# First unit's diagonal blocks from whole key products, and most gate columns made beside the mixture

## The chip, the cores and the metric

The kernel runs on one core of one Trainium2 chip. The metric is the device time of one execution in microseconds (us), median over runs. TensorE (PE, with its weight loads PEld), VectorE (DVE), ScalarE (ACT) and GpSimd (POOL) compute; SyncE (SP) issues most DMAs.

## What is computed

A linear attention with a delta rule (4 batches, 8 heads, 768 tokens, 48 wide), then a dense layer with a squared rectifier, then a mixture of experts of which each token takes one or none. Only the first two matter here:

```python
k_n = k / (norm(k) + 1e-6)
for t in range(768):
    y[t] = q[t] @ state
    v_old = k_n[t] @ state
    state = state + b[t] * outer(k_n[t], v[t] - v_old)
h = x @ w_in                      # x: 3072 x 384, d_ff 2048
x = (max(h, 0) ** 2) @ w_out      # next: skip and gate scores of x, experts
```

## The kernel before

**Units and chunks.** The sequence is cut into 12 chunks of 64 tokens, two to a unit, six units. In a unit the 16 pairs of head and batch halves and the two chunks make four jobs, `ci` 0 to 3 (two chunks by two halves of heads). For each chunk the recurrence becomes a triangular system of 64x64 per head; its two diagonal blocks of 32x32 are inverted on VectorE for all heads at once (`sysinv`, 31 steps of two operations, L394 and L395, on a tile that has one block per partition), and the off-diagonal block is joined in by small products (`merge`). `recur` then carries the state through the chunks (KS, R, U, Uc, Y, Yc, DS, DSv). Its output `xf` is moved into place by SP (L600) and split into a high and a low half, `xh` (L811) and `xl` (L814), which feed the dense layer. The text calls that layer the mixture: per unit 16 pieces of 128 columns of `w_in`, each a product `h` (L828), activations, and a product `y` (L858).

**The first unit.** Before anything, key and query tiles are loaded (L274). `diag` makes the diagonal blocks straight in PSUM in the layout that a transpose needs: per job 64 small products of a 32-wide block with 16 columns, scattered at a stride of 32 elements, into two banks that stay open over all four jobs. `turn` transposes each bank on VectorE (L359) into `Asys`. `both` makes the products of keys with keys and with queries, and `copy` brings them to SBUF as `G` and `P` on ScalarE (L309, L310). The norms of the keys come from squares on ScalarE (L506), `n2` and `rest` on VectorE (L510 on, tile `nw`), and a multiply on POOL (L519). POOL also masks `P` (L525).

**The weight pieces.** A piece comes as raw 64-bit data (L664) in a ring of four buffers and is converted: `size` on ScalarE (L672), `tail`, `join`, `sign` on VectorE (L676, L681, L685). Then its gate columns, ten more columns of `w_out` times the gate weights, are made: x1 (three transposes, L691), x1c (copy, L695), x2 (three products, L700), x2c (copy, L703). x1c of a piece waits for x2 of the piece before. The opening has nine such pieces, the other seven come in the first unit's mixture. A piece is then split into a high half (L784) and a low half (L788), gate columns included, ahead of its `h`.

**The order.** A planner in the program (`Order`) writes the order of all engines. A job has an urgency (lower goes first), an engine, a planned duration, and jobs that it waits for; each engine takes, among the jobs that are ready within 0.35 us of the earliest, the most urgent. While TensorE has no job in the opening, it puts in dummy products (L1432). The opening is planned until a list of jobs is done (L1460); then the jobs of the mixture are added and planned. Urgencies of the opening: `diag` -400, squares and norms -360 + ci (K0), inversion -350, `both` -200, recurrence R0 = -30 and up, merges MG = -30 + ci, pieces -25 + 2p and up, gate columns at most -10 and up.

Of the kernel before, what the change touches and what calls it, by code (L numbers as in the profile page):

```python
# [8 lines left out]
F32 = mybir.dt.float32  # L9
# [7 lines left out]
PE, ACT, DVE, POOL, SP = ET.PE, ET.Activation, ET.DVE, ET.Pool, ET.SP  # L17
# [2 lines left out]
NO, NR, NQ, CL = 9, 2, 16, 14.0  # L20
GAP = 1.5
U1, V0, C0, CS, CX = 20.0, 0.0, -25.0, 2.0, -10.0
K0, R0, MG = (-360.0, 1.0), (-30.0, 5.0, 2.0), -30.0
S1 = 100.0, 1.0
DL = 3.0
NWR = 6
# [9 lines left out]
B, H, S, D = 4, 8, 768, 48  # L36
# [162 lines left out]
class Attn:  # L199
# [32 lines left out]
    def init(s, pool):  # L232
        s.q0, s.LT0, s.QP0 = ([pool.tile(sh, F32, name=f"{n}0{i}") for i in range(2)] for n, sh in (("gkq", [128, 8, 128]), ("lt", [128, 2, 8, 64]), ("qp", [128, 2, 8, 64])))
        s.Tn0 = pool.tile([128, 32, 32], F32, name="tn0")
        s.one = pool.tile([1, 1], F32, name="root")
        s.nc.vector.memset(s.one, 1.0)
        s.b0 = pool.tile([128, 32], F32, name="b0")
        s.nc.gpsimd.dma_start(out=s.b0, in_=s.bs[0])
# [18 lines left out]
    def gram(s, i, ci):  # L257
        nc = s.nc
        c, h8 = i * 2 + ci // 2, ci % 2 * 8
        st = {}  # L260

        def load():
            st["q"] = s.gq[ci % 2]
            for a in range(2):
                nc.sync.dma_start(out=st["q"][a * 64:a * 64 + D].rearrange("p a b -> p (a b)"), in_=s.kq[c, a, :, h8 * 128:(h8 + 8) * 128])

        if i == 0:
            t = (s.q0[ci] if ci < 2 else s.gq[ci % 2]).rearrange("p a b -> p (a b)")
            kt, qt = (t[:, x * 512:x * 512 + 512] for x in range(2))
            k3, q3 = (x.rearrange("p (a b) -> p a b", b=64) for x in (kt, qt))  # L270

        def load0(x):
            for a in range(2):
                (nc.sync if x or not a else nc.scalar).dma_start(out=(kt, qt)[x][a * 64:a * 64 + D], in_=(s.kf, s.qf)[x][c, a, :, h8 * 64:(h8 + 8) * 64])  # L274

        def diag():
            if ci == 0:
                s.dg = [s.psum([128, 16, 32]) for u in range(2)]
            for p in range(8):
                for a in range(2):  # L280
                    f = 64 - a * 64
                    for j in range(2):
                        o = a * 64 + j * 32
                        for u in range(2):
                            nc.tensor.matmul(s.dg[u][o:o + 32, :, ci * 8 + p], lhsT=k3[f:f + D, p, j * 32:j * 32 + 32], rhs=k3[f:f + D, p, j * 32 + u * 16:j * 32 + u * 16 + 16], start=True, stop=True, tile_position=(f, o))

        def both():
            s.P[0, ci], s.G[0, ci] = s.pP.tile([128, 8, 64], F32, name="P"), s.pG.tile([128, 8, 64], F32, name="G")
            st[0], st[1] = s.psum([128, 4, 128]), s.psum([128, 4, 128])
            for q in range(4):  # L290
                for b in range(2):
                    for x in (k3, q3):
                        for a in range(2):
                            f, o = 64 - a * 64, (x is q3) * 64
                            nc.tensor.matmul(st[b][a * 64:a * 64 + 64, q, o:o + 64], lhsT=k3[f:f + D, 2 * q + b], rhs=x[f:f + D, 2 * q + b], start=True, stop=True, tile_position=(f, a * 64))

        def mm():
            s.P[i, ci] = s.pP.tile([128, 8, 64], F32, name="P")
            s.G[i, ci] = s.pG.tile([128, 8, 64], F32, name="G")
            st[0], st[1] = s.psum([128, 4, 128]), s.psum([128, 4, 128])  # L300
            for q in range(4):
                for b in range(2):
                    for a in range(2):
                        f = (1 - a ^ b) * 64
                        nc.tensor.matmul(st[b][a * 64:a * 64 + 64, q, :], lhsT=st["q"][f:f + D, 2 * q + b, 0:64], rhs=st["q"][f:f + D, 2 * q + b, :], start=True, stop=True, tile_position=(f, a * 64))

        def copy(b):
            P, G, gp = s.P[i, ci], s.G[i, ci], st[b]
            nc.scalar.copy(out=G[:, b::2], in_=gp[:, :, 0:64])  # L309
            nc.scalar.copy(out=P[:, b::2], in_=gp[:, :, 64:128])  # L310

        def store(js=(0, 1)):
            G = s.G[i, ci]
            if i not in s.A:
                s.A[i] = s.dram.tile([128, 32, 32], F32, name="Ad")
            for j in js:
                for a in range(2):
                    r = ((j * 4 + ci) * 2 + a) * 8
                    g = G[a * 64 + j * 32:a * 64 + j * 32 + 32, :, j * 32:j * 32 + 32]
                    nc.sync.dma_start(out=s.A[i][r:r + 8].rearrange("p s t -> s p t"), in_=g)  # L320

        if i == 0:
            return [(SP, 0.5, lambda: load0(0), 0.8), (PE, 2.4, diag, 4, 0, 2) if ci == 0 else (PE, 2.4, diag), (SP, 1.0, lambda: load0(1), 0.8), (PE, 2.0, both, 1, 2048, 2), (ACT, 0.77, lambda: copy(0)), (ACT, 0.77, lambda: copy(1))]
        w, d = (3.6, 2.9) if i == 1 else (1.9, 0.8)
        return [(SP, 1.0, load, 1.3), (PE, 1.0, mm, 1, 1536, 2), (ACT, 0.77, lambda: copy(0)), (ACT, 0.77, lambda: copy(1)), (SP, w, store, d)]

# [16 lines left out]
    def sysinv(s, i):  # L343
        nc = s.nc
        v = nc.vector
        st = {}

        def prep():
            st["A"] = s.c1.tile([128, 32, 32], F32, name="Asys")
            st["b"] = s.p2.tile([128, 32], F32, name="bsys") if i else s.b0  # L350
            st["w"] = s.p2.tile([128, 4, 32], F32, name="wsys")
            if i:
                nc.sync.dma_start(out=st["b"], in_=s.bs[i])
                nc.sync.dma_start(out=st["A"], in_=s.A.pop(i))

        def turn(u):
            if u == 0:
                prep()
            v.transpose(out=st["A"][:, u * 16:u * 16 + 16], in_=s.dg[u])  # L359

        def turn1():
            v.transpose(out=s.Tn0, in_=st["X"].rearrange("p t s -> p s t"))
# [46 lines left out]
        if i:  # L409
            head = [(SP, 1.0, prep, 1.7)]  # L410
        else:
            head = [(DVE, 0.65, lambda u=u: turn(u)) for u in range(2)]
        head += [(DVE, 0.95, n0), (DVE, 0.2, n1), (ACT, 0.25, lambda: st["root"]()), (DVE, 3.1, n2)]
        steps = [(DVE, (0.45 if i else 0.29) + 2 * (31 - k) * (k + 1) / 960, lambda k=k: step(k)) for k in range(31)]
        return head + steps + ([(SP, 0.5, store2, 0.9), (DVE, 1.95, fin1), (SP, 0.5, store1, 1.7)] if i else [(DVE, 1.6, turn1), (DVE, 1.9, turn2)])
# [911 lines left out]
def schedule(A, open_V, open_M, clear, E, free, ca, tail, ew, manual):  # L1327
    o = Order()
    o.use({"a": 3, "y": 4})
    free[0] = o  # L1330
    gr, si, kv, mg, rc = {}, {}, {}, {}, {}


    def at(d, m, *k):
        x = d.get(m)
        for j in k:
            x = x and x[j]
        return [] if x is None else [x]

    def gram(i, c, ul, u, b=()):  # L1340
        m, l = 4 * i + c, A.gram(i, c)
        old = at(gr, m - 2, 5)
        if i == 0:
            x = [o.add(ul + 10, l[2], [], at(gr, m - 1, 0) + list(b))] * 3
            q = o.add(u, l[3], x[:1], at(gr, m - 1, 5) + sd)
            c0 = o.add(u, l[4], [q])
            gr[m] = x + [q, c0, q, o.add(u, l[5], [q, c0])]
            return
        x = [o.add(ul, l[0], old, at(gr, m - 1, 0) + list(b))]
        x += [x[0]] * 2  # L1350
        q = o.add(u, l[1], x[:1], at(gr, m - 1, 5) + at(mg, m - NG, -4) + at(kv, m - NP, 6))
        c0 = o.add(u, l[2], [q])
        c1 = o.add(u, l[3], [q, c0])
        gr[m] = x + [q, c0, q, c1] + [o.add(u, z, [c1]) for z in l[4:]]

    def sysinv(i, u):
        l, x = A.sysinv(i), []
        n = len(l)
        for k in range(n):
            if i == 0:  # L1360
                w = sd[-1:] + x[-1:] if k < 2 else [] if k == 2 else x[-2:] if k == 3 else x[-1:]
            elif k == n - 2:
                w = x[-2:-1]
            else:
                w = x[-1:] if x else [j for c in range(4) for j in gr[4 * i + c][7:]] + at(si, i - 1, -1)
            x.append(o.add(u(k), l[k], w, at(si, i - 1, -2)))
        si[i] = x
# [40 lines left out]
    made, cc, lo = [], [], {}  # L1408
# [21 lines left out]
    with A.tc.tile_pool(name="st", bufs=1, side="right") as pool:  # L1430
# [3 lines left out]
        sd, l0 = [], [A.gram(0, c) for c in range(4)]  # L1434
        ld = []
        for l in l0:
            ld.append(o.add(-400, l[0], [], ld[-1:]))
        o.add(-398, (ACT, 1.5, A.warm), [], ld[-1:])
        for c in range(4):
            sd.append(o.add(-400, l0[c][1], ld[c:c + 1], sd[-1:]))  # L1440
        sysinv(0, lambda k: -350)
        made += [o.add(-140, l) for l in A.init2()]
        for c in range(4):
# [13 lines left out]
        cl = o.add(200, (SP, 0.5, clear, 0.6), [cc[-1][0]], at=170)  # L1457
        for c in range(2):
            keys(1, c, 100 + c, 110 + c)
        o.run(rc[2][2] + rc[3][2] + rc[2][3] + rc[3][3] + [x[-2] for x in cc] + gr[7])  # L1460

    manual.close()
    M = open_M()
# [9 lines left out]
    a = o.taken["a"]  # L1473
# [101 lines left out]
    ld = {}  # L1575
# [60 lines left out]
```

## Time and profile before

| | us |
|---|---|
| median of 3 runs | 894.8 |
| lowest and highest | 889.54, 895.5 |
| profiled execution | 882.78 |
| its span | 881.0 |
| TensorE busy | 831.3 (94%) |
| VectorE busy | 550.2 (62%) |
| ScalarE busy | 489.4 (56%) |
| POOL busy | 205.2 (23%) |

The rows come from one profiled execution, and times in them count from the start of its span. A row of the timeline gives start, duration, engine, source line, operation, output and input tile, and in brackets how long the engine was idle before and what ended that. Matmuls of 32-bit numbers appear as two records each.

### The profile page before, as it was taken

To read this page: it belongs to the slowest core of one execution; us is meant where nothing else is said; L and a number is where in the kernel's file an instruction comes from. 1 tells how busy PE (TensorE), PEld (TensorE's weight loads), DVE (VectorE), ACT (ScalarE), POOL (GpSimd) and SP (SyncE) were. 2 spreads that over 40 slices of the span, in tenths; PEclk is the share of its full clock that TensorE was granted. 3 is DMA by queue.
4 is the path that set the end of the run, shared out by engine and by line. 5 is a ranking of instruction groups with operands and counts; after the bars stand their busy time and mean duration, and the time that the engine had idled before them with its cause. 6 is when DMAs were issued, how large, how long until landed. Compare 5 with 4: busy or idle time off the path is not lost. (4 is left out here: it accounts for less than half of the span.)

```text
span 881.0 us, 24628 instructions
## 1 busy us (share of the span) xinstructions
PE 831.3 (94%) x9410; PEld 722.3 (82%) x9410; DVE 550.2 (62%) x1267; ACT 489.4 (56%) x997; POOL 205.2 (23%) x325
## 2 busy tenths in 40 slices
PE   5988799999999998999999999999999999999996
PEld 4867677887788887888788888898998789998995
DVE  5998899678767885875688543216425226744763
ACT  2448366767556475556765585546643226643651
POOL 6403501132213324232132412002302401111111
PEclk9987599999999998999999999999999999999999
DMA  7446367846675576347663553227702426535661
GB/s 239 161 109 208 112 193 224 237 124 209 176 191 132 152 212 178 106 130 174 186 160 113 155 142 108 96 78 240 275 0 76 140 95 226 208 109 186 215 218 32
DMA packets 112794, 139.24 MB, mean 158 GB/s; under 512 B 65064, under 2 KB 82969, under 8 KB 112656
## 3 DMA queue, kind: packets, MB, share of 16 engines
q1 hardware_dynamic: 103888, 118.15, 45.0%
q0 software_dynamic: 8192, 18.54, 6.6%
q8 instruction: 78, 1.28, 0.6%
q10 hardware_dynamic: 576, 0.79, 0.3%
q14 instruction: 60, 0.49, 0.2%
HBM read 108.55 MB, written 29.88 MB: 157 GB/s over the span
## 5 line engine op out<-in xcount | busy, mean ns | idle before, releaser
L844 DVE TENSOR_TENSOR gl<-g,gh 128x512 fp32r<-128x512 f32 x96 | 67.8, 707 | 114.6 <-ACT gh L837 114.4
L833 ACT ACTIVATE r<-p_h 128x512 f32<-128x512 f32 x96 | 57.3, 597 | 144.1 <-PE p_h L828 144.0
L519 POOL TENSOR_TENSOR x<-x,nw 64x384 f32<-64x384 f32 x48 | 44.5, 926 | 139.8 <-DVE nw L338 131.3
L395 DVE TENSOR_TENSOR Xsys<-Xsys,Osys 128x31 f32<-128x31 f32 (+15 forms) x186 | 69.7, 375 | 6.2
L394 DVE TENSOR_TENSOR Osys<-Asys,Xsys 128x31 f32<-128x31 f32 (+15 forms) x186 | 70.5, 379 | 4.1
L525 POOL TENSOR_SCALAR_AFFINE_SELECT qp<-P 64x512 f32<-64x512 f32 x48 | 37.2, 775 | 133.6 <-PE p_a L592 123.2
L931 POOL DMA_INDIRECT xs<-x2s,di x24 | 25.1, 1046 | 171.6 <-DVE emx L966 65.8
L841 ACT ACTIVATE g<-r 128x512 f32<-128x512 f32 x96 | 60.6, 632 | 6.5 <-DVE gl L844 3.9
L858 PE MATMUL p_y<-wk,gh 128*128 128x394 f32 x288 | 64.2, 345 | 0.0
L828 PE MATMUL p_h<-xh,wk 128*128 128x512 f32 x216 | 63.0, 401 | 0.7 <-DVE wk L788 0.7
L1200 POOL DMA_INDIRECT out<-eo,ex x21 | 23.6, 1123 | 162.8 <-DVEq L1098 94.3
L837 ACT CAST gh<-g 128x512 fp32r<-128x512 f32 x96 | 59.6, 621 | 2.9
L1194 PE MATMUL ey<-w2h,egh 128*128 128x384 f32 x168 | 58.3, 347 | 1.5 <-ACTq L1098 1.3
L1194 PE MATMUL ey<-w2l,egh 128*128 128x384 f32 x168 | 56.6, 337 | 1.5 <-issue 1.5
L858 PE MATMUL p_y<-wraw,gh 128*128 128x394 f32 x240 | 57.6, 362 | 0.0
L828 PE MATMUL p_h<-xh,wraw 128*128 128x512 f32 x180 | 54.6, 411 | 2.7 <-ACT r L833 2.7
L1194 PE MATMUL ey<-w2h,egl 128*128 128x384 f32 x168 | 56.7, 338 | 0.2
L1172 ACT ACTIVATE eg<-eh 128x512 f32<-128x512 f32 x42 | 23.0, 597 | 59.7 <-PE eh L1170 59.3
L858 PE MATMUL p_y<-wraw,gl 128*128 128x394 f32 x240 | 53.6, 346 | 0.0
L858 PEld LDWEIGHTS p_y<-wk,gh 128*128 128x128 f32 x288 | 53.1, 191 | 0.0
L828 PE MATMUL p_h<-xl,wraw 128*128 128x512 f32 x180 | 52.3, 398 | 0.1
L828 PEld LDWEIGHTS p_h<-xh,wk 128*128 128x128 f32 x216 | 41.4, 192 | 10.6 <-DVE wk L788 1.1
(267 smaller groups left out, 1958.0 us busy)
## 6 DMA issues: line engine op xcount, KB each, us to landing
wraw<-wh SPq DMA_DIRECT2D x60, 389.0 KB, 3.7
raw<-in_w SPq DMA_DIRECT2D x16, 768.0 KB, 4.8
r<-in_w SPq DMA_DIRECT2D x24, 512.0 KB, 4.8
r<-in_w SPq DMA_DIRECT2D x32, 384.0 KB, 5.3
wraw<-wc SPq DMA_DIRECT2D x20, 389.0 KB, 3.6
gkq<-in_kq SPq DMA_DIRECT2D x40, 192.0 KB, 3.6
wh<-whi SPq DMA_DIRECT2D x12, 389.0 KB, 3.6
ex<-xs SPq DMA_DIRECT2D x24, 193.0 KB, 2.5
```

Of the source, the lines that this page charges most:

```text
L394: v.tensor_tensor(out=tmp, in0=A[:, k, k + 1:32].unsqueeze(2).to_broadcast(sh), in1=X[:, k, None, 0:k + 1].to_broadcast(sh), op=ALU.mult)
L395: v.tensor_tensor(out=X[:, k + 1:32, 0:k + 1], in0=X[:, k + 1:32, 0:k + 1], in1=tmp, op=ALU.subtract)
L519: nc.gpsimd.tensor_tensor(out=x, in0=x, in1=st["n"][r].unsqueeze(2).to_broadcast([64, 8, D]), op=ALU.mult)
L525: nc.gpsimd.affine_select(out=QP[r, 1 - t], in_=P[r], pattern=[[0, 8], [1, 64]], compare_op=ALU.is_gt, fill=0.0, base=0, channel_multiplie ...
L828: nc.tensor.matmul(ps, lhsT=w[:, k * 128:k * 128 + 128], rhs=x[k], start=(n == 0), stop=(n == 8))
L833: nc.scalar.activation(out=r, in_=st["p"], func=AF.Relu)
L837: nc.scalar.copy(out=s.g[f][0], in_=st["g"])
L841: nc.scalar.activation(out=g, in_=st["r"], func=AF.Square)
L844: nc.vector.tensor_tensor(out=s.g[f][1], in0=st["g"], in1=s.g[f][0].bitcast(F32), op=ALU.subtract)
L858: nc.tensor.matmul(s.ys[t], lhsT=g[:, t * 128:t * 128 + 128], rhs=w[:, DM:], start=first, stop=last)
L931: return s.nc.gpsimd.indirect_dma_start(out=s.xs, out_offset=bass.IndirectOffsetOnAxis(ap=idx, axis=0), in_=src, in_offset=None, bounds_ch ...
L1194: nc.tensor.matmul(y, lhsT=g[:, f, :], rhs=w[:, f, :], start=(i == 0), stop=(i == 23))
```

## The change

The products of the diagonal blocks are gone. `keys` makes the whole 64x64 products of keys with keys of a job; `part(0)` on ScalarE and `part(1)` on VectorE copy the two diagonal blocks of it into an SBUF tile `Gd`, `off` copies the off-diagonal block to `G`; `scores` makes the products with the queries and `copy0` copies them to `P`. `turn` transposes all of `Gd` at once. `keys` and the two parts have urgency -400 + c, `off` -390 + c, `scores` -200 + c. R0 goes from -30 to -40. The opening's list of jobs asks for the sign of all nine pieces and for the gate columns of the first four, where it asked for the gate columns of all nine.

```diff
-K0, R0, MG = (-360.0, 1.0), (-30.0, 5.0, 2.0), -30.0
+K0, R0, MG = (-360.0, 1.0), (-40.0, 5.0, 2.0), -30.0
...
+        s.Gd = pool.tile([128, 32, 32], F32, name="gd")
...
-        def diag():
...
-                        for u in range(2):
-                            nc.tensor.matmul(s.dg[u][o:o + 32, :, ci * 8 + p], lhsT=k3[f:f + D, p, j * 32:j * 32 + 32], rhs=k3[f:f + D, p, j * 32 + u * 16:j * 32 + u * 16 + 16], start=True, stop=True, tile_position=(f, o))
...
+        def keys():
+            st["k"] = s.psum([128, 8, 64])
             for p in range(8):
                 for a in range(2):
                     f = 64 - a * 64
...
+                    nc.tensor.matmul(st["k"][a * 64:a * 64 + 64, p], lhsT=k3[f:f + D, p], rhs=k3[f:f + D, p], start=True, stop=True, tile_position=(f, a * 64))
+
+        def part(j):
+            for a in range(2):
+                o = a * 64 + j * 32
+                (nc.vector.tensor_copy if j else nc.scalar.copy)(out=s.Gd[o:o + 32, ci * 8:ci * 8 + 8], in_=st["k"][o:o + 32, :, j * 32:j * 32 + 32])
+
+        def off():
+            s.G[0, ci] = s.pG.tile([128, 8, 64], F32, name="G")
+            for r in (0, 64):
+                nc.scalar.copy(out=s.G[0, ci][r:r + 32, :, 32:64], in_=st["k"][r:r + 32, :, 32:64])
+
+        def scores():
+            st["s"] = s.psum([128, 8, 64])
...
+        def copy0():
+            s.P[0, ci] = s.pP.tile([128, 8, 64], F32, name="P")
+            nc.scalar.copy(out=s.P[0, ci], in_=st["s"])
...
-            return [(SP, 0.5, lambda: load0(0), 0.8), (PE, 2.4, diag, 4, 0, 2) if ci == 0 else (PE, 2.4, diag), (SP, 1.0, lambda: load0(1), 0.8), (PE, 2.0, both, 1, 2048, 2), (ACT, 0.77, lambda: copy(0)), (ACT, 0.77, lambda: copy(1))]
+            return [(SP, 0.5, lambda: load0(0), 0.8), (SP, 1.0, lambda: load0(1), 0.8), (PE, 1.1, keys, 3, 1024), (ACT, 0.7, lambda: part(0)), (DVE, 0.7, lambda: part(1)), (ACT, 0.7, off), (PE, 1.1, scores, 1, 1024), (ACT, 0.6, copy0)]
...
-        def turn(u):
-            if u == 0:
-                prep()
-            v.transpose(out=st["A"][:, u * 16:u * 16 + 16], in_=s.dg[u])
+        def turn():
+            prep()
+            v.transpose(out=st["A"], in_=s.Gd.rearrange("p s t -> p t s"))
...
-            head = [(DVE, 0.65, lambda u=u: turn(u)) for u in range(2)]
+            head = [(DVE, 1.95, turn)]
...
+        dg = []
         for c in range(4):
-            sd.append(o.add(-400, l0[c][1], ld[c:c + 1], sd[-1:]))
+            l = l0[c]
+            sd.append(o.add(-400 + c, l[2], ld[c:c + 1], sd[-1:]))
+            dg += [o.add(-400 + c, z, sd[-1:]) for z in l[3:5]]
+            of = o.add(-390 + c, l[5], sd[-1:])
...
-        o.run(rc[2][2] + rc[3][2] + rc[2][3] + rc[3][3] + [x[-2] for x in cc] + gr[7])
+        o.run(rc[2][2] + rc[3][2] + rc[2][3] + rc[3][3] + [x[4] for x in cc] + [x[-2] for x in cc[:4]] + gr[7])
```

## Rows read from the trace of the kernel before

**Rows 1.** The page's slices of the span, 40 equal ones, tenths.

```profile
PE   5988799999999998999999999999999999999996
```

**Rows 2.** Windows: stretch, length, busy of PE, PEld, DVE, ACT, POOL, clock, DMA, GB/s.

```profile
22.84:59.06 36.22, 31.16 (x503) 27.52 (x501) 33.78 (x79) 14.09 (x41) 10.11 (x15) 0.96 0.48 128
59.06:91.10 32.04, 27.47 (x716) 23.11 (x714) 27.85 (x49) 24.09 (x59) 11.55 (x19) 0.77 0.56 184
91.10:106.47 15.37, 12.96 (x84) 11.14 (x84) 11.96 (x28) 8.58 (x24) 8.17 (x62) 0.50 0.36 108
106.47:160.00 53.53, 49.45 (x406) 41.52 (x403) 49.79 (x113) 33.48 (x65) 4.62 (x4) 0.96 0.70 202
```

**Rows 3.** TensorE's timeline from 4.5, instruction packets 7.93 to 19.5, window of L295.

```profile
4.58 3.36 PE L285 MATMUL p_a<-gkq 48*32 48x16 f32 x216
10.82 1.95 PE L285 MATMUL p_a<-gkq 48*32 48x16 f32 x128 [2.89 <-issue]
...
q8 instruction: 3, 0.05, 2.0%
...
19.57:24.55 4.98, 4.96 (x88) 4.87 (x89) 1.00 1.02 356
```

**Rows 4.** ScalarE's timeline at 7.8; groups by line (busy us, mean ns), 59 to 91.

```profile
7.78 0.20 ACT L241 ACTIVATE root<-root 1x1 f32<-1x1 f32 x1
...
L595 ACT COPY xf<-p_y 128x512 f32<-128x512 f32 x3 | 1.8, 587 | 0.2
L454 ACT COPY Z<-p_y 32x256 f32<-32x256 f32 x5 | 1.8, 365 | 0.1
```

**Rows 5.** VectorE: norms (window, tile nw), a transpose by line, two in the timeline.

```profile
8.00:23.00 15.00, 6.67 (x24) 1.00 0.85 266
...
L362 DVE STREAM_TRANSPOSE tn<-Xsys 128x1024 f32<-128x1024 f32 x1 | 1.9, 1900 | 0.0
...
22.84 1.31 DVE L359 STREAM_TRANSPOSE Asys<-p_a 128x512 f32<-128x512 f32 x2
```

**Rows 6.** The steps: window of tile Osys, two steps, POOL in the timeline and by line.

```profile
28.64:55.33 26.69, 24.57 (x62) 1.00 0.49 115
...
28.65 0.68 DVE L394 TENSOR_TENSOR Osys<-Asys,Xsys 128x31 f32<-128x31 f32 x1
...
107.03 0.19 DVE L394 TENSOR_TENSOR Osys<-Asys,Xsys 128x31 f32<-128x31 f32 x1
...
23.46 2.47 POOL L519 TENSOR_TENSOR x<-x,nw 64x384 f32<-64x384 f32 x2 [3.16 <-DMA x<-in_kv]
...
28.64 2.78 POOL L525 TENSOR_SCALAR_AFFINE_SELECT qp<-P 64x512 f32<-64x512 f32 x4
...
L519 POOL TENSOR_TENSOR x<-x,nw 64x384 f32<-64x384 f32 x8 | 7.3, 910 | 7.7 <-DVE nw L338 4.2 <-DMA x<-in_kv 3.2
```

**Rows 7.** Window of tile raw on VectorE.

```profile
59.06:91.10 32.04, 19.73 (x24) 0.77 0.56 184
```

**Rows 8.** Timeline of the mixture's start, several engines.

```profile
90.14 0.96 DVE L685 SCALAR_TENSOR_TENSOR wk<-raw,wk 128x768 uint32<-128x768 uint32 x1
...
94.03 0.62 ACT L811 CAST xh<-xf 128x512 fp32r<-128x512 f32 x1 [0.57 <-DMA xf<-xf]
...
99.88 0.96 DVE L788 TENSOR_TENSOR wk<-wk,whi 128x778 fp32r<-128x778 f32 x1
...
106.47 1.65 PE L828 MATMUL p_h<-xh,whi 128*128 128x512 f32 x3
106.65 0.36 DVE L572 TENSOR_TENSOR x<-x,p_a 64x192 f32<-64x192 f32 x1 [3.05 <-PE p_a L565]
...
111.43 0.36 DVE L572 TENSOR_TENSOR x<-x,p_a 64x192 f32<-64x192 f32 x1 [1.33 <-PE p_a L565]
```

**Rows 9.** A later piece's gate columns beside the mixture, TensorE's timeline.

```profile
118.07 0.52 PE L691 MATMUL p_a<-idn,cvo 128*128 128x128 f32 x3 [0.98 <-PE p_y L858]
...
120.49 0.73 PE L700 MATMUL p_a<-sg,cvt 128*128 128x10 f32 x6
```

More of the change, by code (lines that the diff above doesn't have):

```diff
@@ L274, in load0 @@
                 (nc.sync if x or not a else nc.scalar).dma_start(out=(kt, qt)[x][a * 64:a * 64 + D], in_=(s.kf, s.qf)[x][c, a, :, h8 * 64:(h8 + 8) * 64])
-        def diag():
-            if ci == 0:
-                s.dg = [s.psum([128, 16, 32]) for u in range(2)]
+        def keys():
+            st["k"] = s.psum([128, 8, 64])
             for p in range(8):
@@ L281, in diag @@
                     f = 64 - a * 64
-                    for j in range(2):
-                        o = a * 64 + j * 32
-                        for u in range(2):
-                            nc.tensor.matmul(s.dg[u][o:o + 32, :, ci * 8 + p], lhsT=k3[f:f + D, p, j * 32:j * 32 + 32], rhs=k3[f:f + D, p, j * 32 + u * 16:j * 32 + u * 16 + 16], start=True, stop=True, tile_position=(f, o))
[L287 to L295, printed above, removed]
+                    nc.tensor.matmul(st["k"][a * 64:a * 64 + 64, p], lhsT=k3[f:f + D, p], rhs=k3[f:f + D, p], start=True, stop=True, tile_position=(f, a * 64))
[9 more added lines that the diff above has]
+            st["s"] = s.psum([128, 8, 64])
+            for p in range(8):
+                for a in range(2):
+                    f = 64 - a * 64
+                    nc.tensor.matmul(st["s"][a * 64:a * 64 + 64, p], lhsT=k3[f:f + D, p], rhs=q3[f:f + D, p], start=True, stop=True, tile_position=(f, a * 64))
+        def copy0():
+            s.P[0, ci] = s.pP.tile([128, 8, 64], F32, name="P")
+            nc.scalar.copy(out=s.P[0, ci], in_=st["s"])
         def mm():
@@ L1340, in gram @@
     def gram(i, c, ul, u, b=()):
-        m, l = 4 * i + c, A.gram(i, c)
+        m, l = 4 * i + c, A.gram(i, c) if i else [l0[c][1]] + l0[c][6:]
         old = at(gr, m - 2, 5)
         if i == 0:
[L1344 to L1347, printed above, removed]
+            x = [o.add(ul + 10, l[0], [], at(gr, m - 1, 0) + list(b))] * 3
+            q = o.add(u, l[1], x[:1], at(gr, m - 1, 5) + sd)
+            gr[m] = x + [q, q, q, o.add(u, l[2], [q])]
             return
@@ L1360, in sysinv @@
             if i == 0:
-                w = sd[-1:] + x[-1:] if k < 2 else [] if k == 2 else x[-2:] if k == 3 else x[-1:]
+                w = dg if k == 0 else [] if k == 1 else x[-2:] if k == 2 else x[-1:]
             elif k == n - 2:
```

## The prediction

> **What bounds the kernel now.** I read the slices of the span first. TensorE is 90% busy or more nearly everywhere but at the left edge [rows 1]. So what the first 107 us save can reach the end, and work that is moved from there into the rest costs its TensorE time. Then I cut the left edge into stretches by the stage that runs in them [rows 2]. From 22.84 to 59.06 VectorE inverts the first unit's systems (33.78 of 36.22 us busy). From 59.06 to 91.10 the recurrence and the weight pieces run, VectorE 27.85 of 32.04, ScalarE 24.09. From 91.10 to 106.47 nothing is full and the clock is 0.50: the gate columns are made one after another. From 106.47 to 160 the mixture runs with TensorE and VectorE both at 93%. What sets the start of the mixture is VectorE's row of work up to 91.10, and behind it TensorE's row of gate columns.
>
> Third, the diagonal blocks. The 512 small records of L285 are 8.1 us of work, but take from 4.58 to 19.66, because TensorE stops three times, waiting for nothing that the profile names: first after 216 records, in the middle of a job of 128, then after every 128, and the instruction queue brings three packets in that time [rows 3]. So it is out of instructions, not of keys. The transposes begin on VectorE at 22.84 [rows 5].
>
> **The change, part by part.** *The blocks on TensorE.* `diag` goes (512 records), `both` (256) is split into `keys` and `scores`, 128 each. Whole products of this kind took 4.96 us for 88 records [rows 3], 0.056 each, so `keys` is 1.8 us a chunk and four are done by 4.58 + 7.2 = 11.8 at the latest. 216 records ran before the first stop, and `keys` needs 128, so no stop lies on this path. Removed: 19.66 - 11.8 = 7.9 us of TensorE, which is not yet a gain, since others become late.
>
> *The copies.* New on ScalarE per chunk: `part(0)` two copies and `off` two, 32x256 out of PSUM, nearest row 0.37 us, and one 128x512, nearest row 0.59 [rows 4]; on VectorE two of 32x256 from PSUM, which the trace doesn't show; between 0.19 (its 128x31 step) and 0.69 (its transpose of 128x512 out of PSUM, 1.31 for two) [rows 5, 6]; I take 0.37, ScalarE's row of the same shape. By the urgencies in the code ScalarE serves part (-400 + c) and off (-390 + c) before the squares of the key norms (-360 + c), and in the order that readiness gives, twelve copies come before the last `part(0)` ends: 12 x 0.37 = 4.4 us behind the table load and its square root, which end at 7.98 [rows 4]. The turn can start at 12.4, not at 11.8. VectorE's own eight copies (3.0 us, 5.5 at the upper bound) lie in that wait, where it has little else: nothing on the path; without that cover they would cost their 3.0.
>
> *What is now late.* Before, the norms of the keys (`n2`, `rest`) were done while VectorE waited for the blocks: 6.67 us of its work between 8 and 23 [rows 5]. Now the squares stand behind twelve to sixteen copies on ScalarE, so `n2` of chunk 0 can't run before the turn, and being more urgent than the inversion (-360 against -350) the four norms go in between the turn and the early steps. Behind them on VectorE wait the steps, and POOL's multiplies L519 wait for each norm. So they come onto the path in full.
>
> *The turn.* One transpose of 128x1024 instead of two of 128x512: 1.90 by the row of the same size, against 1.3 [rows 5].
>
> *The sum to the end of the inversion.* 12.4 + 1.9 turn + 6.7 norms + 4.5 from turn to first step (from the end of the transposes, 22.84 + 1.31, to 28.65) [rows 5, 6] + 26.7 steps + 3.8 two transposes [rows 5, 6] = 56.0. To this a term for POOL: the step on 128x31 takes 0.68 with POOL's selects beside it and 0.19 without [rows 6]; two of POOL's eight multiplies (0.91 each) came after the turn, at 23.46; the six others now fall into the chain too. Bounds: 0, if they meet operations that they don't delay, and 6 x 0.91 = 5.5, if each is waited for in full; a select cost about 0.5 when it met a step, so half of that would be 3; but some of them meet the other norms, and the 6.67 were measured with multiplies beside them. I take 1.0. End: 57.0 against 59.06, 2 us earlier.
>
> *The recurrence and the pieces.* Before, one of the nine pieces was done ahead of 59.06, eight after it [rows 7]. Now all nine come behind the inversion: eight pieces took 19.73 of VectorE between 59.06 and 91.10 [rows 7], so a ninth is 2.5. The last sign ends at 57.0 + 32.0 + 2.5 = 91.5 against 91.10. R0 from -30 to -40 lets the recurrence's operations go before merges and pieces; it changes who waits, not VectorE's sum. I take it as nothing, since the split of xf (xh) came behind the last sign anyway [rows 8]; if ScalarE starves the pieces' `size` it costs up to the 4.2 us that VectorE idled there.
>
> *The gate columns.* Each is a transpose (0.52), a copy, a product (0.73) and a copy [rows 9], with one buffer between them, so they run one behind the other; at the clock of 0.50 [rows 2] I put a piece at twice 0.52 + 0.73, 2.5 us. No DMA hangs on those of the opening, since their store is empty. The first mixture product waited for them: its inputs were ready when the low half of the first weight was, at 99.88 + 0.96 = 100.84, and it began at 106.47 [rows 8]. With five of nine pieces no longer demanded before it, it can begin 91.5 + 9.74 = 101.2: 5.3 us earlier. Work given back: at that pace 5.3 / 2.5, two pieces, are left by then, 2 x 1.25 = 2.5 us beside the mixture. TensorE gains 2.8. VectorE's waits of 3.05 and 1.33 us for TensorE in that stretch [rows 8] go too: 4.4, less 0.4 for the later sign, 4.0. Both engines are at 93% behind it, so I take the middle: 3.4 us.
>
> The profiled execution took 882.78 us, of which 881.0 span; it would become 879.4. Three executions had a median of 894.8, 12 us above the profiled one, so there the same gain gives 891.4.
>
> **A rule weighed.** VectorE's 128x31 product took 0.68 us beside POOL's select and 0.19 alone [rows 6]. The Trainium skill ("SBUF — State Buffer", section "Who interferes with whom") says that a VectorE instruction with two SBUF inputs and a GpSimd instruction that reads SBUF exclude each other, the loser blocked for the whole instruction, and that one that only writes doesn't count. The rows agree: 0.68 is about the length of one select, 2.78 for four. By the rule each multiply is waited for in full, and the sum would have 5.5 in place of 1.0.
>
> **Rivals.** *B, a gain three times as large.* The norms run before the turn after all, or in waits of the chain (ScalarE faster, or the squares let in). For it: ScalarE is free from 7.98 on [rows 4], and before the change all four norms were done by 23 in the waits of others [rows 5]. Against it: twelve copies of more urgent jobs. Then 6.7 us leave the chain: the inversion ends at 50.3, the last sign at 84.8, the first product at 94.5, 12.0 earlier; less 2.5 on TensorE is 9.5, on VectorE 6.3 + 4.4 = 10.7: 10 us, 884.8. Chance 0.22.
>
> *C, POOL eats it.* All six multiplies are waited for in full: the inversion ends 4.5 later than I say, the sign at 96.0, the first product at 105.7. TensorE gains 0.8 with no piece left, VectorE loses 0.5: 0.2 us, 894.6. For it: 24.57 us of steps in 26.69 [rows 6], some at three times their clean length. Against it: POOL waits for a DMA before its last multiplies. Chance 0.20.
>
> *D, slower: the mixture waits for its weights.* The five late pieces need x1, x1c, x2, x2c, high and low half before their product; these stand in ScalarE's queue among the mixture's own activations. If a piece isn't ready when its turn comes, TensorE stops for a pace of 2.5 us and works 1.25: five pieces are 18.8 us, less the 5.3 gained is 13.5 late, 908.3. It decides from two stopped pieces on (7.5 > 5.3). For it: a later piece's transpose did stop TensorE by 0.98 [rows 9]. Against it: only the fifth piece onward is late, and the products of four pieces stand before it on TensorE. Chance 0.10.
>
> The rest, 0.05, is the planner: the order of all later work is laid out anew from other start times, by some us of either sign.
>
> **The numbers.** My forecast, 891.4, has 0.43, with its own range from 887 to 897 (POOL's term from 0 to 3, the pieces given back from none to five, ScalarE's share). 8 in 10 asks for C whole and most of B: 882 to 899; D and the lower tail of B stay out. About 1% (8.9 us) is what a measurement of this kernel can tell from no change: faster means under 885.9, slower over 903.7. Faster: half of B and more, 0.15, and 0.06 from the forecast and the planner: 0.21. Slower: D, 0.08, and the planner: 0.10. Same: 0.69.
>
> **What would show it.** In the new profile: `keys` without a stop, done by 12; the transpose of 128x1024 at 12 to 13; the four norms behind it and not ahead; first step near 25, not 19; last transpose ending at 55 to 59; last sign at 90 to 93; first mixture product near 101 with two or three transposes of pieces behind it. Wrong at the norms if the first step comes before 21; wrong at POOL's term if steps above 0.6 us number more than twenty; wrong at the gate columns if the first product still waits for them, or if TensorE shows waits of a us and more for the halves of the fifth to ninth weight.

## The result and the profile after

| | before | after |
|---|---|---|
| median of 20 runs each, one chip, us | 889.52 | 896.95 |
| lowest and highest, us | 881.98, 897.19 | 892.75, 901.52 |
| profiled execution, us | 882.78 | 899.56 |
| its span, us | 881.0 | 897.8 |

The changed kernel takes 1.0078 of the time before, 95% interval 1.0055 to 1.0101. In a later run, where before has a median of 899.8, the ratio was 1.0034 [1.0005, 1.0062]. So it is 2 to 7 us slower where the prediction said 3.4 us faster. The move is under 1%, but the sign was wrong. That 896.95 lies in the predicted range of 882 to 899 says little: the prediction started from 894.8, a median of three runs of before, whose median is 889.52 here and 897.8 to 899.8 on the chips of the later runs.

The first part went as predicted. This is the timeline of after, several engines (start, duration, engine, line, operation, tiles, count, idle before with its releaser):

```profile
4.57 3.89 PE L282 MATMUL p_a<-gkq 48*64 48x64 f32 x96
8.29 1.10 PE L282 MATMUL p_y<-gkq 48*64 48x64 f32 x32
...
13.51 1.93 DVE L366 STREAM_TRANSPOSE Asys<-gd 128x1024 f32<-128x1024 f32 x1 [0.86 <-ACT gd L287]
15.58 0.55 DVE L517 TENSOR_REDUCE nw<-sq 128x8 f32<-128x384 f32 x1
...
23.55 0.18 DVE L401 TENSOR_TENSOR Osys<-Asys,Xsys 128x31 f32<-128x31 f32 x1
...
29.57 0.89 DVE L401 TENSOR_TENSOR Osys<-Asys,Xsys 128x135 f32<-128x135 f32 x1
...
55.99 1.91 DVE L373 STREAM_TRANSPOSE Asys<-Xsys 128x1024 f32<-128x1024 f32 x1
```

The 128 whole products run to 9.39 without the stops of [rows 3]. The turn is at 13.51, the norms stand behind it, the first step comes at 23.55, and the last transpose ends at 57.90, 1.2 us earlier than the 59.06 of before [rows 2].

Then the windows (stretch, length, busy of PE, PEld, DVE, ACT, POOL, clock, DMA share, GB/s) show a hole that before doesn't have [rows 2]:

```profile
57.90:70.43 12.53, 11.47 (x296) 9.09 (x298) 10.96 (x16) 11.44 (x32) 0.56 (x1) 0.77 0.04 12
70.43:80.45 10.02, 2.46 (x92) 2.13 (x84) 0.00 (x0) 1.69 (x4) 3.65 (x7) 0.67 0.83 250
80.45:102.53 22.08, 15.18 (x342) 13.39 (x342) 19.39 (x36) 11.86 (x25) 5.61 (x7) 0.59 0.63 202
102.53:113.79 11.26, 8.52 (x42) 7.88 (x43) 9.43 (x28) 6.55 (x19) 10.50 (x65) 0.63 0.33 107
```

From 70.43 to 80.45 VectorE does nothing at all, and the DMA engines, idle in the 12 us before (share 0.04), are 83% busy. The timeline says what it waits for, and what stands behind the waiting instruction:

```profile
70.86 0.81 ACT L447 COPY lt<-Asys 32x256 f32<-32x256 f32 x2
80.51 0.94 ACT L679 ACTIVATE raw<-raw 128x768 f32<-128x768 f32 x1 [8.33 <-DMA raw<-in_w]
...
80.45 0.56 DVE L683 TENSOR_SCALAR raw<-raw 128x768 uint32<-128x768 uint32 x1 [10.03 <-DMA raw<-in_w]
80.93 1.50 DVE L624 TENSOR_TENSOR x<-x,p_a 48x192 f32<-48x192 f32 x4
...
101.25 1.28 DVE L692 SCALAR_TENSOR_TENSOR wk<-raw,wk 128x768 uint32<-128x768 uint32 x1
...
107.77 1.15 ACT L818 CAST xh<-xf 128x512 fp32r<-128x512 f32 x2
...
113.79 1.63 PE L835 MATMUL p_h<-xh,whi 128*128 128x512 f32 x3
```

Four of nine pieces are converted by 70.43, as many as the ring holds. The fifth hasn't been loaded, and the recurrence's own operation (DSv, L624) stands behind the piece's in VectorE's order. Last sign at 102.53 (before 91.10), first mixture product at 113.79 (before 106.47) [rows 8]. Why the loads were late, SP's timeline of after shows:

```profile
48.39 0.45 SPq L361 DMA_DIRECT2D bsys<-in_bs  x1
48.94 1.30 SPq L266 DMA_DIRECT2D gkq<-in_kq  x3
71.70 0.35 SPq L362 DMA_DIRECT2D Asys<-Ad  x1
72.10 12.71 SPq L671 DMA_DIRECT2D raw<-in_w  x5
```

SP stands from 50.2 to 71.70 before the load of the second unit's systems, `Asys`. That load overwrites the tile from which the last `place` copies the first unit's inverses (L447, ending at 71.67 above). SP's waits say so too (who waited for whom: us in total, times, longest):

```profile
SPq L362 <- ACT lt L447: 13.8, 1, 13.8
```

The 7.5 us ahead of that went to the last transpose of the inversion (L373). Five raw loads stand behind the load of Asys and are then issued in one bunch. While VectorE stands, the recurrence's next product on TensorE (KS) waits for the DSv that is queued behind the piece:

```profile
81.33 2.24 PE L572 MATMUL p_y<-x,lt 48*64 48x48 f32 x32 [8.41 <-DVE x L624]
```

SP's row of before:

```profile
61.46 5.38 SPq L664 DMA_DIRECT2D raw<-in_w  x3
66.89 0.44 SPq L353 DMA_DIRECT2D bsys<-in_bs  x1
72.79 0.33 SPq L354 DMA_DIRECT2D Asys<-Ad  x1
73.18 0.41 SPq L664 DMA_DIRECT2D raw<-in_w  x1
```

There SP issued three of the five from 61.46, ahead of bsys and Asys, and one behind; the first had come at 25. In the DMA issues of the stretch (count, KB each, median us from issue to landing), after first, before second:

```profile
raw<-in_w SPq DMA_DIRECT2D x6, 768.0 KB, 12.1
```

```profile
raw<-in_w SPq DMA_DIRECT2D x4, 768.0 KB, 4.3
```

The order was turned by the planner. In the planner's own reckoning (planned times, not those of a trace), before, the stores of the second unit's blocks kept SP busy to 56.5; then the raw loads, far more urgent, were ready first. After, the stores are out by 46.1 and landed at 51.0, which makes `prep` ready, the job with both loads. The first ring buffer is free only at 53.05, so `prep` is taken, though less urgent. The planner knows the stores that Asys needs, but not that its tile is still being read.

### The profile page after: what moved, and what is told of

The parts are those of the page before. It is cut to its first block, busy times and chain, and to the rows that moved or that the text cites. A ratio compares the mean times of both kernels' runs of the same rounds, so it can differ in the third digit from the quotient of the medians.

```text
span 897.8 us, 23901 instructions
## 1 busy us (share of the span) xinstructions
PE 838.9 (93%) x9035; PEld 728.9 (81%) x9035; DVE 556.9 (62%) x1274; ACT 490.5 (55%) x1001; POOL 205.4 (23%) x325
## 3 DMA queue, kind: packets, MB, share of 16 engines
q1 hardware_dynamic: 103888, 118.15, 44.6%
## 5 line engine op out<-in xcount | busy, mean ns | idle before, releaser
L402 DVE TENSOR_TENSOR Xsys<-Xsys,Osys 128x31 f32<-128x31 f32 (+15 forms) x186 | 72.3, 389 | 6.4
L1201 PE MATMUL ey<-w2l,egh 128*128 128x384 f32 x168 | 56.5, 336 | 0.0
```

The source lines that it names most:

```text
L402: v.tensor_tensor(out=X[:, k + 1:32, 0:k + 1], in0=X[:, k + 1:32, 0:k + 1], in1=tmp, op=ALU.subtract)
L1201: nc.tensor.matmul(y, lhsT=g[:, f, :], rhs=w[:, f, :], start=(i == 0), stop=(i == 23))
```

## The experiments

All ratios are against the kernel before on the same chip, with 95% intervals. The runs used three chips: one for e1 to e4, one for e5, e6 and the changed kernel once more, one for e7 to e10. Two kernels on different chips are compared through their ratios; the ratio of one kernel differed between chips by 0.3% (e1 and e10) and 0.4% (the changed kernel). The theory (Q in the quoted texts): SP's order costs the time. The rivals: the gate columns beside the mixture (D), POOL and the norms (C), R0.

**One load later (e1).** The changed kernel; only `prep` moves, behind the raw loads.

```diff
+        for x in cc[4:8]:
+            o.link(si[1][0], x[0])
         cl = o.add(200, (SP, 0.5, clear, 0.6), [cc[-1][0]], at=170)
```

> The changed kernel, with one order more: the load of the second unit's systems (bsys, Asys) is issued only behind the raw loads of the fifth to eighth weight piece. Nothing else moves in the planned order of any engine. Theory Q (SP's queue): the 10.03 us in which VectorE stood before the fifth piece's tail go, the raw loads land 4 to 5 us after their issue again instead of 12, the last sign comes at 92 to 93 instead of 102.5, the first mixture product at 102 to 105 instead of 113.8, and the time falls by 7 to 11 us against the changed kernel: 886 to 890 where before measures 889.5, a ratio of 0.996 to 1.000. Rival D (the gate columns beside the mixture cost the time): the stop goes and the sign comes earlier, but the mixture stands still for its weights, and the ratio stays over 1.004. Rival C (norms and POOL): the sign comes earlier by less than 5 us.

0.9904 [0.9868, 0.9940], median 892.8. Run once more on another chip (e10), 0.9931 [0.9904, 0.9957]. The 10 us stop is gone; SP, VectorE, ScalarE and TensorE in the timeline:

```profile
60.29 5.25 SPq L671 DMA_DIRECT2D raw<-in_w  x3
72.00 9.46 SPq L671 DMA_DIRECT2D raw<-in_w  x3
81.98 0.47 SPq L362 DMA_DIRECT2D Asys<-Ad  x1
...
89.28 0.90 ACT L679 ACTIVATE raw<-raw 128x768 f32<-128x768 f32 x1 [5.96 <-DMA raw<-in_w]
90.20 1.33 ACT L593 COPY x<-p_a 64x192 f32<-64x192 f32 x4
...
95.53 1.29 DVE L692 SCALAR_TENSOR_TENSOR wk<-raw,wk 128x768 uint32<-128x768 uint32 x1
...
109.18 1.63 PE L835 MATMUL p_h<-xh,whi 128*128 128x512 f32 x3
```

The gain is larger than expected (0.996 to 1.000), the stage came later: last sign at 96.82 (93.62 in the second run), not 92 to 93, and first product at 109.18 (105.05), not 102 to 105. So this kernel is 6 to 9 us faster than before although its first product comes near that of before (106.47 and 106.84), once later and once earlier. The loss went with the load's place; by which path the gain over before reaches the end, no run shows. A smaller stop of the same kind is left: ScalarE stands 5.96 us for the ninth raw load, and the recurrence's last copies (L593) stand behind it.

**The second half alone (e2).** Before, with R0 at -40 and the new list.

```diff
-        o.run(... + [x[-2] for x in cc] + gr[7])
+        o.run(... + [x[4] for x in cc] + [x[-2] for x in cc[:4]] + gr[7])
```

> The kernel before with the change's second half alone: the opening ends with the signs of all nine pieces and the gate columns of the first four, and R0 is -40. The diagonal blocks are as before. Theory Q: the raw loads stay ahead of the second unit's load, except for the last piece, so no stop of VectorE; inversion ends at 59, last sign at 90 to 92, first mixture product at 100 to 103 instead of 106.5; TensorE has 2 to 5 pieces' gate columns (1.25 us each) beside the mixture; 2 to 4 us faster than before, ratio 0.995 to 0.998. Rival D: products wait for later weights' halves, stops over 1 us on TensorE between 103 and 130, and the ratio is 1.004 or more. Rival R0 (the reordered recurrence starves the pieces): the last sign is later than 93.

0.9962 [0.9935, 0.9990]. Last sign 91.00, first product 103.47. No stop of TensorE for a weight was over 1.4 us. Rival D is out for this half; R0, which moved with it, is taken alone below.

**The first half alone (e3).** After, with the old list and R0 at -30.

> The changed kernel with the change's second half taken back: all nine pieces' gate columns are demanded before the mixture, R0 is -30; the whole products, copies and the one transpose stay. Theory Q: inversion ends at 57.9 as in the changed kernel, the second unit's load still stands ahead of five raw loads, VectorE stops 8 to 11 us before the fifth piece, last sign at 101 to 103, and the first mixture product, 15 us behind the sign as before, at 114 to 118: ratio 1.008 to 1.014, that is no better than the changed kernel. Rival D: without the late gate columns the loss is gone, ratio 1.000 or less. Rival R0: with -30 the stop before the fifth piece is under 4 us.

1.0114 [1.0081, 1.0148]. Last sign 103.62, first product 120.57, and SP as in after:

```profile
73.03 0.35 SPq L362 DMA_DIRECT2D Asys<-Ad  x1
73.42 11.97 SPq L671 DMA_DIRECT2D raw<-in_w  x5
```

The loss is in this half, though its own inversion ends earlier than before's.

**The first half with one load later (e8).** e3's kernel and e1's two lines.

> The changed kernel's first half alone (whole products, copies, one transpose) with the raw loads first; all nine pieces' gate columns are demanded before the mixture and R0 is -30, as in before. It differs from e3_blocks_only by the order of one load alone, and from e7_r30 by the demanded gate columns alone. Theory Q: e3's ratio of 1.011 falls by the stop of about 10 us, to 0.998 to 1.002, with the inversion at 57.9 and the first product at 104 to 109; the gate columns are then worth the difference to e7_r30, 3 to 7 us. If the stop is not what e3 lost, the ratio stays over 1.006.

0.9988 [0.9961, 1.0015]. The raw loads go first again:

```profile
70.68 6.00 SPq L671 DMA_DIRECT2D raw<-in_w  x2
77.77 0.43 SPq L362 DMA_DIRECT2D Asys<-Ad  x1
```

Against 1.0114 that is 1.26%, 11 us, for the place of one job in SP's order, more than the intervals and the 0.4% between chips. In the orders that the planner writes for e3 and e8, all jobs of all engines stand in the same place over the whole program but this one job on SP; the same holds for the changed kernel and e1. So the cause of the loss is shown by two pairs, and the gate columns are no part of it. By itself the first half, with the loads in time, is worth 1 us, which can't be told from nothing.

**The loads late in the kernel before (e4).** Before, with the raw loads from the fifth piece on behind the second unit's load.

```diff
-        b = [g0]
+        b = [g0] + (si[1][:1] if 4 <= p < NO else [])
```

> The kernel before with one order more: the raw loads of the fifth to ninth piece are issued only behind the load of the second unit's systems, as the changed kernel has it; nothing else of the change. Theory Q: the load of Asys waits on SP for the last copy of the first unit's inverses (72 to 73), five raw loads come bunched behind it and land 8 to 12 us after their issue; VectorE stands 6 to 10 us before the fifth piece; last sign at 97 to 101 instead of 91.1; 5 to 9 us slower than before, ratio 1.006 to 1.010. If SP's queue is not the cause: ratio within 0.997 to 1.003.

0.9966 [0.9932, 1.0000]: a miss. The loads were late as in after (Asys at 73.13, four raw loads in a bunch), and the engines waited for them:

```profile
ACT raw L672 <- DMA raw<-in_w: 5.8, 5, 4.4
DVE raw L676 <- DMA raw<-in_w: 0.3, 1, 0.3
```

Last sign 96.86, first product 110.14, 3.3 us later than in the second trace of before (106.84, on another chip). Yet the time didn't rise. What differs from after: VectorE waited 0.3 us for a raw load and not 10, and its last DSv ended at 90.77 (before 90.48, after 99.56). The edit moved more than SP's row. Here the planner reckons with the late loads and lays out the other engines anew: on VectorE a DSv of the recurrence (L617) now stands ahead of the fifth piece's first step, where in after it stands behind (80.93 above):

```profile
72.03 1.47 DVE L617 TENSOR_TENSOR x<-x,p_y 48x192 f32<-48x192 f32 x4 [2.28 <-PE p_y L609]
79.20 0.56 DVE L676 TENSOR_SCALAR raw<-raw 128x768 uint32<-128x768 uint32 x1 [0.28 <-DMA raw<-in_w]
```

So late loads needn't cost time: here they cost nothing that the runs can tell, in the changed kernel 11 us, with the recurrence queued behind them. That it is the recurrence's delay, rather than the pieces', that reaches the end is argued from this comparison, not shown: no run moved the DSv alone.

**R0 (e7).** e1's kernel with R0 at -30.

> The changed kernel with the raw loads first, and R0 back at -30: the recurrence's operations no longer go before the merges' placing copies. Only R0 differs from e1_loads_first. Theory Q says R0 is no part of the loss: ratio 0.987 to 0.994, last sign within 4 us of 96.8. Rival R0 (the new order of recurrence and merges on ScalarE and TensorE matters by itself): the first mixture product moves by over 4 us from 109.2 and the ratio leaves 0.985 to 0.996.

0.9911 [0.9880, 0.9942], like e1. R0 is no part of the loss. Against e8 it differs by the list alone: 0.9911 to 0.9988, so the gate columns beside the mixture are worth some 7 us here, more than the 3.4 of e2. Why more is open.

**The norms ahead of the turn (e5, e9).** e1's kernel with

```diff
-K0 = (-360.0, 1.0)
+K0 = (-410.0, 1.0)
...
-            of = o.add(-390 + c, l[5], sd[-1:])
+            of = o.add(-340 + c, l[5], sd[-1:])
```

> The changed kernel with the raw loads first (as in e1_loads_first), and the key norms of the first unit put ahead of the later diagonal copies: their urgency from -360 to -410, that of the copies into G from -390 to -340. So ScalarE makes the squares between the copies, and three of the four norms are planned ahead of the turn. Theory N (the norms were 6.7 us of the chain behind the turn, as the prediction says): the turn comes 1 to 2 us later, the first step at 19 to 22, the steps run without norms among them and the last transpose ends at 52 to 55 instead of 57.9; last sign and first product 3 to 5 us earlier than in e1_loads_first; time 2 to 5 us below it, ratio 0.984 to 0.988. Theory P (POOL: its multiplies fall on the steps whatever the order, each waited for): the last transpose ends at 56.5 to 58, and the ratio is that of e1_loads_first, 0.990.

0.9895 [0.9856, 0.9935]. The turn moved to 16.49, the first step to 25.73, the steps ran without norms among them, and the last transpose ended at 55.57 instead of 57.88. Moving the norms there was worth 2.3 us, not 6.7: the steps took 26.1 us from first to last instead of 30.6, but the turn came 3.0 us later, with two of the norms and part of the third ahead of it. The first product came at 100.22, 9 us earlier than in e1, but the time hardly fell, so both were run again on one chip.

> e5_norms_first once more, beside e1_loads_first on one chip. In its trace the first unit's scores are copied at 214.5 against 223.4 in e1_loads_first, 8.9 us earlier, yet the whole span was only 3.5 us shorter, and the ratios were 0.9895 and 0.9904. If the 5.4 us between were lost to chance in the last stage (the experts took 220.8 us behind the last unit there, 214 to 219 elsewhere), this run is 4 to 9 us faster than e10_loads_again, ratio 0.980 to 0.987. If a start that is earlier by 9 us is given back further on whatever the run (a later wait sets the end), it is within 3 us of e10_loads_again again, and its last stage is over 219 us again.

> e1_loads_first once more, as the partner of e9_norms_again on the same chip. Theory Q expects 0.987 to 0.994 again, and the first unit's scores at 222 to 225.

0.9940 [0.9913, 0.9966] and 0.9931 [0.9904, 0.9957]: no difference again. In both profiled executions the norms-first kernel reaches the end of the sixth unit 3 to 8 us ahead and then loses 5 us in the experts (220.8 and 220.5 us to the end, against 215.9 and 215.5). Most of it is lost at one place in both. TensorE at its last expert, norms first (e5, e9), then loads first (e10):

```profile
877.80 0.69 PE L1201 MATMUL ey<-w2h,egh 128*128 128x384 f32 x1 [3.77 <-issue]
```

```profile
879.38 0.47 PE L1201 MATMUL ey<-w2h,egh 128*128 128x384 f32 x1 [4.44 <-ACTq L1268]
```

```profile
878.69 0.41 PE L1201 MATMUL ey<-w2h,egh 128*128 128x384 f32 x1 [0.80 <-ACTq L1105]
```

This is where the program leaves the chain of `If`s. The stop is 0.75 to 1.38 us in the other traces (before, e2 and e4 have another of 1.5 to 1.8 behind it). The last products behind it are slower too, 5.60 us for 23 records at a clock of 0.70 (e9), against 4.31 for 24 at 1.00 (e10; windows, columns as above):

```profile
879.40:885.00 5.60, 5.60 (x23) 5.60 (x24) 0.00 (x0) 0.00 (x0) 0.00 (x0) 0.70 0.02 6
```

```profile
877.90:883.00 5.10, 4.31 (x24) 4.11 (x24) 1.29 (x2) 0.71 (x2) 0.97 (x1) 1.00 0.19 55
```

**The remaining stop of e1 (e6).** e1's kernel with the raw load planned at 4.0 us.

```diff
-        return [(SP, 0.5, load, 2.5)] + wide + ...
+        return [(SP, 0.5, load, 4.0)] + wide + ...
```

> The changed kernel with the raw loads first, and with each raw load given 4.0 us instead of 2.5 in the order's plan. What it changes: ScalarE's first step of the last two pieces (size) is put behind the recurrence's copies, and VectorE's work on them with it. In e1_loads_first ScalarE stood 5.96 us before the ninth piece's size, for its load, with the last copies of the recurrence queued behind it, TensorE stood 4.32 and the last Yc came at 91.6 to 95.0. Theory Q (an in-order queue that stands before a load holds up the recurrence): that wait moves behind the recurrence, the last Yc comes at 88 to 91, xh 3 to 6 us earlier than 103.2, the first product at 104 to 107 and the time is 2 to 5 us below e1_loads_first, ratio 0.984 to 0.989. Rival: the pieces themselves set the first product, not the recurrence: first product at 108 to 110 and a ratio of 0.989 to 0.993.

1.0022 [0.9993, 1.0052], no faster than the changed kernel on the same chip (1.0034): a miss, though the stage did what the theory said. The last Yc came at 89.0 instead of 94.4, the first product at 105.31 instead of 109.18. The gain went at the second unit's start, where the mixture's first product came at 236.84 and in e1 at 229.80, with a wait of its own (SP, then TensorE):

```profile
217.43 7.78 SPq L607 DMA_DIRECT2D xf<-xf  x6
226.40 4.11 SPq L328 DMA_DIRECT2D Ad<-G  x8
233.61 4.08 SPq L266 DMA_DIRECT2D gkq<-in_kq  x4
...
234.82 2.10 PE L313 MATMUL p_a<-gkq 48*64 48x128 f32 x32 [10.36 <-DMA gkq<-in_kq]
236.84 1.65 PE L835 MATMUL p_h<-xh,wraw 128*128 128x512 f32 x3
```

The mixture's product could have run from 227.3, when its xh was ready, but the third unit's key product stood ahead of it on TensorE, and its load behind the moves and stores on SP. It looks like the same pattern, 150 us on. But the longer planned load also laid out the later orders anew (SP issues eight stores ahead of these key loads, in e1 four), so this run doesn't test the stop alone. What it shows is that a gain in the opening can be lost again behind it.

**Both kernels once more**, on the chip of e5 and e6:

> The kernel before once more, unchanged, so that its trace comes from the same chip and hour as the experiments. The trace of before that the prediction was read from took 882.78 us, at the low end of its runs. Every theory expects the same left edge (inversion ends at 59, last sign at 91, first mixture product at 106 to 107); if the profiled time is 890 to 900, the rest of the difference lies behind 107 us, in stretches that no theory about the opening speaks of, and the traces of the experiments have to be held against this one there.

> The changed kernel once more, unchanged, on the chip of the others. All theories expect what it did before: a stop of about 10 us of VectorE before the fifth piece, last sign at 102 to 103, first mixture product at 113 to 115, ratio 1.005 to 1.011. With it the gain of loading first is read as a difference on one chip.

Before took 896.09 in that execution, with the same left edge (last sign 91.47, first product 106.84). After is the 1.0034 above. Runs of one kernel spread over 3 to 15 us, so one trace bears out where a stop is, not a gain of a few us. The table puts the single executions side by side, of before and after these second ones; the scores of a unit (copied behind its last product) are a mark of TensorE's progress. The last column is the ratio of the runs, not of the two spans.

| kernel | first product | longest stop of TensorE, 107 to 300 | scores of unit 1 | unit 3 | unit 6 | span | ratio to before |
|---|---|---|---|---|---|---|---|
| before | 106.84 | 4.6, gkq | 216.43 | 423.74 | 676.49 | 894.3 | 1 |
| after | 113.24 | 5.9, xh | 230.15 | 435.14 | 681.85 | 897.2 | 1.0034 |
| loads first (e1) | 109.18 | 5.8, xh | 223.39 | 431.41 | 677.91 | 893.8 | 0.9904 |
| the same (e10) | 105.05 | 6.5, xh | 220.09 | 427.04 | 673.35 | 888.8 | 0.9931 |
| norms first (e5) | 100.22 | 1.8, xh | 214.53 | 422.95 | 669.47 | 890.3 | 0.9895 |
| the same (e9) | 101.95 | 1.4, cvo | 216.92 | 423.18 | 670.60 | 891.1 | 0.9940 |
| late size (e6) | 105.31 | 10.4, gkq | 221.55 | 436.68 | 683.11 | 898.7 | 1.0022 |
| R0 -30 (e7) | 108.69 | 1.6, r | 220.86 | 426.92 | 673.35 | 888.8 | 0.9911 |
| first half, loads first (e8) | 110.13 | 1.5, cvt | 222.53 | 424.30 | 672.45 | 889.2 | 0.9988 |
| second half (e2) | 103.47 | 5.8, ex | 216.56 | 425.45 | 674.00 | 893.1 | 0.9962 |
| first half (e3) | 120.57 | 2.8, cvt | 239.32 | 443.81 | 692.86 | 909.2 | 1.0114 |
| loads late in before (e4) | 110.14 | 4.1, gkq | 222.49 | 433.20 | 679.48 | 898.1 | 0.9966 |

The first product explains part of the order only: e1 and e10 are behind before at the first unit's end and faster all the same. After is 13.7 us behind before at the first unit's end, 5.4 at the sixth's and 2.9 at the end. The largest part comes back in the fifth unit (85.5 us in that trace of before, 80.8 in after). Before itself took 79.9 there in the trace that the prediction was read from, so this is a spread between executions and no property of the change.

## Why the prediction was right or wrong

*The blocks on TensorE, the copies, the turn: right.* `keys` was done by 9.39 without a stop (said: by 11.8). VectorE's copy of 32x256 took 0.43 (taken as 0.37). The turn was at 13.51 (said 12.4), 1.93 long (1.90).

*What is now late: right in place, too large as a lever.* The norms stood behind the turn, as said, and first step and end of inversion were 23.55 and 57.90 (said 25 and 57.0). That the end came out so near is partly luck: from turn to first step it took 8.1 us where the sum had 11.2, and from first step to last 30.6 where it had 27.7, since part of the norms ran among the steps. Rival B priced their removal at 6.7 us; e5, which moved them ahead of the turn, measured 2.3.

*POOL's term: right in kind, a little small.* Of 62 step operations 12 took over 0.6 us (8 before). The prediction's bar was twenty. The 62 took 26.30 us of VectorE, 1.7 more than before, where 1.0 was taken. The Trainium skill's rule ("SBUF — State Buffer", section "Who interferes with whom") agrees with these rows: steps beside POOL's multiplies and selects take 0.68 to 0.89, the two of 128x60 beside a fill, which only writes, 0.22. What the whole rule made of the sum, 5.5 us, didn't come, since four of the eight multiplies met steps and the others met norms and the preparation of the first step.

*The recurrence and the pieces: this step failed.* It said that all nine pieces behind the inversion cost one piece's VectorE time, 2.5 us, and put the last sign at 91.5; it came at 102.53. From the inversion's end to the last sign the sum had 34.5 us and it took 44.6, of which VectorE stood 10.03 for a load; with the loads ahead it took 38.9 (e1) and 35.7 (e10). The sum counted VectorE and took the loads as there. It was right that no piece is done before the inversion's end now; what follows from it was missed: the fifth piece's raw load, which came at 25 before, falls into the stretch behind the inversion, and which load SP issues there was never asked. SP's row of before showed bsys and Asys among the raw loads, three ahead and one behind, and Asys waiting until 72.79. Those lines carried the risk. The step should have asked what happens to the raw loads if Asys comes ahead of them.

*The gate columns: right in sign, about twice too large.* In e2, where no stop intervenes, the first product came at 103.47, 12.5 us behind the last sign. Before it was 15.4 behind, so 2.9 us were gained where the sum had 5.6 (9.74 behind). In after, seven of nine pieces still had their gate columns made in front of the first product, between 99.29 and 113.79, since its xh came late as well (107.77). Rival D fell: no product of the mixture waited for a weight by more than 1.1 us in after, e1, e2 or e7.

*R0 as nothing: right* (e7, with the loads first).

*The numbers.* Where the loads come in time, the second half alone is worth 3.4 us (e2), the first alone about 1, within noise (e8), and both together 6 to 9 (e1, e10), twice the 3.4 forecast. That they are more together than apart is not explained: the prediction's path to it, an earlier first product, didn't come in e1 (109.18, where 101.2 was said). What turned the sign is one term, a loss of some 10 us, that the sum didn't have. It was no rival either: none of them was a load.

## What to carry to other kernels

When a change frees a queue earlier, ask for each in-order queue what is taken next and what that waits for: a load into a buffer still being read stops all loads behind it, and the loads then come in a bunch (12.1 us to land in place of 4.3). In the order of a computing engine, keep work that waits for a load behind the work of the longest chain, since the wait is inherited by all that follows (VectorE 10.03 us here, with the recurrence behind it). In e4 the planner knew that the loads were late, put the recurrence first, and the time didn't rise. A planner with priorities must know of buffer reuse; where it doesn't, an explicit link can stand in for it (11 us here for two lines).

## What was not expected of the hardware

The stop of TensorE at the last branch was 0.75 to 1.38 us in twelve traces, and 3.77 and 4.44 in the two of one kernel whose experts' source is the same. The Trainium skill ("Runtime: NRT & Kernel Launch", section "Instruction fetch mechanics") says that a taken branch whose target lies outside the pages at hand forces a fetch before execution goes on; a stop at that place fits this, but no run here moved the code alone, and why it is longer in this kernel is open. Behind the stop of 4.44 us the granted clock was 0.70 in the window, a mean of its two levels, where e10, with a stop of 0.80, had 1.00 throughout.
